# Spectral mixing and SoLU on one core: quarter-array stays of four units, a later booked landing of transposes, an earlier rank for the last product

## Chip, cores, metric

One core of one Trainium2 chip. The metric is device time in microseconds (us) of one execution; the kernel before was run three times (median 1628.03, 1625.98 to 1630.09), and one more execution was profiled.

## What is computed

```python
X = np.fft.rfft(x, axis=1)                    # x: 8 x 3136 x 256, float32
Yr = X.real @ w_r - X.imag @ w_i + b_r
Yi = X.real @ w_i + X.imag @ w_r + b_i
Y  = soft_threshold(Yr, 0.01) + 1j * soft_threshold(Yi, 0.01)
t  = np.fft.irfft(Y, n=3136, axis=1).reshape(25088, 256)
h  = t @ w_in                                 # 256 -> 1024
solu = h * softmax(h)
ln = (solu - mean) / sqrt(var + 1e-6) * g_ln
out = ln @ w_out                              # 1024 -> 256
```

## The kernel before

Each of the 8 batches goes through two Fourier steps forward (`fwd1`, `fwd2`), the mixing product with threshold (`mix`), two steps back (`inv1`, `inv2`), and then a product with `w_in`, an activation and a product with `w_out`. Products of single precision are made of three float16 products on TensorE: high part by high, high by low, low by high.

**Front.** `fwd1` of batches 2 to 7 works on quarters of the array (49 rows by 64 columns, weights `fa16_s`) with four PSUM banks a stay; batches 0 and 1 use single precision (`fwd1_plain`, weights `fa_s`). Results go to DRAM and come back regrouped. `fwd2`, `mix` and `inv1` work on 13 units a batch: 12 units of two frequency pairs and a last, smaller one. `inv1` contracts over 64 rows, so that two products lie in the array at once, one on each half of its rows (weights `gb`). In batches 1 to 7 it takes two units in one uninterrupted group, 24 matmuls into two banks, and writes one `zout` tile (two buffers), which goes to DRAM in one transfer; `yh` and `yl`, the halves of a mixed unit, have four buffers each. `inv2` brings rows into a ring (`ring_hi`, `ring_lo`) as 128-row tiles of the output.

**Back.** 24 or 25 tiles of 128 rows a batch, 196 in all. `moe_head`: 12 matmuls of 512 columns into two banks (`ph`), row maximum, exponential and product into `u` (four buffers). `moe_turn`: `u` is split into `lh` (ScalarE) and `ll` (GpSimd), two buffers each, and both are transposed by DMA (SyncE's queue) into `th` and `tl`, three buffers each. `moe_tail`: 16 matmuls of 256 columns with `th`, then 8 with `tl`, into one `po` bank; scaled, stored.

**Order.** All instructions are recorded first, and a planner (`Plan.order`, line 351) then writes out the order of every engine by hand; the chip follows that order and waits only on semaphores. The planner books a length for each operation. On each engine it takes, among the operations that could start within 50 ns of the earliest, the one of lowest key, then of earliest recording. Batch `b`'s tile `n` has the keys `first + n` (head), `first + n + 0.5` (turn) and `first + n + 1.5` (tail), where `first` counts the tiles of the batches before. `front_b(b + 1)` is spread over the same keys: unit `n` of `fwd2` and `mix(n - 1)` at `key + n * step`, and the `inv1` of units `u - 1, u` at step `u + 3`; a step is some 1.2 tiles, and 1.0 tile in batch 1. A transpose is booked with 1.6 us of the queue, 1.5 us of a common bus and 2.0 us to land; what depends on it may start then, and the buffers that it reads (`lh`, `ll`) come free then, in the book (lines 414 to 426). Banks: 8 in all, at most 5 for the front (`pf`), 5 for heads, 2 for tails (line 478). Matmuls on parts of the array are booked with 100 ns to enter such a stay from the full array and 220 ns otherwise.

Of the kernel before, what the change touches and what calls it, by code (L numbers as in the profile page):

```python
# [12 lines left out]
F32 = mybir.dt.float32  # L13
F32R = mybir.dt.float32r
BF16 = mybir.dt.bfloat16
F16 = mybir.dt.float16
# [18 lines left out]
LOW = 2.0**11  # L35
# [207 lines left out]
class Plan:  # L243
# [60 lines left out]
    def weigh(self, op, name, args, kw, ins, outs):  # L304
        if name == "dma_start":
            v = next(v for v in (*outs, *ins) if not isinstance(v, DramView))
            size = (v.rows[1] - v.rows[0]) * v.cells.size * mybir.dt.size(v.dtype)
            cross = kw.get("transpose", False)
            op.length += 1600.0 if cross else 430.0
            op.moved += 1500.0 if cross else size / 270.0  # L310
        elif op.engine == "tensor":
            moving = ins[-1]
            n = moving.cells.size * (4 if moving.dtype == F32 else 1) * 0.42 + 1
            name = ins[0].tile.kw["name"]
            op.split = 2 if "gb" in name else 4 if name == "fa16_s" else 1
# [35 lines left out]
    def order(self):  # L351
# [38 lines left out]
        while len(done) < len(self.ops):  # L390
# [22 lines left out]
                port = op.end  # L413
            if op.moved:
                bus = max(bus, op.end) + op.moved
                op.end = bus + 2000.0
            for t in op.tiles:
                if t.owner is None:
                    t.owner = op
# [39 lines left out]
def fft_mix_solu_kernel(ctx: ExitStack, tc, x, w_r, w_i, b_r, b_i, w_in, w_out, g_ln, fa, fbf, fsf, iaf, fa16, fb, fs, gb, gs, ia, out):  # L459
# [29 lines left out]
        return t  # L489

    nc.key = -300
    fa_s = load([N1, N1], fa, "fa_s")
    nc.key = 0
    ident = const.tile([P, P], F32, name="ident")
    ones = const.tile([P, P], F32, name="ones")
# [66 lines left out]
    def set_scales(b):  # L562
# [19 lines left out]
        nc.vector.tensor_scalar(un[:, 3:], un[:, :1], 1.0 / S_SCALE, sc[:, 1:2], ALU.mult, ALU.mult)  # L582
        nc.vector.tensor_scalar(sc[:, 2:3], sc[:, 1:2], LAM, None, ALU.mult)
        nc.vector.tensor_scalar(sc[:, 3:4], sc[:, 1:2], -LAM, None, ALU.mult)
        bias_y = fp.tile([P, 2, D], F32, name="bias_y", bufs=2)
        nc.vector.tensor_scalar(bias_y, bias_t, sc[:, 1:2], None, ALU.mult)
        nc.vector.tensor_scalar(un[:, 2:3], un[:, 3:], w_un, None, ALU.mult)
        scales[b] = dict(
            x=sc[:, 0:1], X=sc[:, 4:], lam=(sc[:, 2:3], sc[:, 3:4]), mix=un[:, 2:3], bias=bias_y, y=un[:, 1:2]
        )  # L590
        if b:
            set_h_scale(b)

# [207 lines left out]
    def mix(b, u):  # L801
        n, _ = unit_size(u)
        half = 2 * N2
        M = n * half
        t = mix_split(b, u) if b else mix_first(u)
        c = fp.tile([P, 2, D], F32, name="yc", bufs=2)
        up, down = scales[b]["lam"]
# [5 lines left out]
        else:  # L813
            nc.vector.tensor_scalar(c[:M], t[:M], up[:M], down[:M], ALU.min, ALU.max)
        nc.gpsimd.tensor_sub(y[:M], t[:M], c[:M])
        yh = fp.tile([P, 2, D], F16, name="yh", bufs=4)
        yl = fp.tile([P, 2, D], F16, name="yl", bufs=4)
        nc.scalar.copy(yh[:M], y[:M])
        nc.gpsimd.tensor_sub(yl[:M], y[:M], yh[:M])
        Ys[b, u] = yh, yl  # L820
# [1 line left out]
    def inv1(b, u0, u1):  # L822


        n, _ = unit_size(u0)
        half = 2 * N2
        K = half * n
        g, gi = divmod(2 * u0, QG)
        part, dtype = ((2, D), F16) if b >= PLAIN_Z else ((D,), F32)
        if n == 1:  # L830
            zo, gi = fp.tile([K, 1, *part], dtype, name="zs", bufs=1), 0
        else:
            if gi == 0:
                zouts[b] = fp.tile([P, QG, *part], dtype, name="zout")
            zo = zouts[b]
        w = u1 - u0
        pz = [front_psum(b) for _ in range(n)]
        nc.reserve(zo[:, gi : gi + n * w])
        with nc.together():
            for u in range(u0, u1):  # L840
                yh, yl = Ys.pop((b, u))
                for k, (t, j) in enumerate(((yh, 0), (yl, 0), (yh, 1))):
                    for ri in range(2):
                        for i in range(n):
                            rows = slice(i * half, (i + 1) * half)
                            gw = gs_s[:, ri, j] if n == 1 else gb_s[g][rows, u % 2, ri, j]
                            nc.tensor.matmul(
                                pz[i][:K, (u - u0) * D : (u - u0 + 1) * D], gw, t[rows, ri], start=k + ri == 0, stop=k + ri == 3
                            )
        m = n * w  # L850
        for i in range(n):
            pv = pz[i][:K, : w * D].rearrange("p (u e) -> p u e", u=w)
            if b < PLAIN_Z:
                zv = zo[:, gi : gi + m].rearrange("p (u i) e -> p u i e", i=n)[:, :, i]
                nc.scalar.activation(zv, pv, AF.Copy, scale=Z_SCALE)
                continue
            zv = zo[:, gi : gi + m].rearrange("p (u i) t e -> p u i t e", i=n)[:, :, i]
            nc.scalar.activation(zv[:, :, 0], pv, AF.Copy, scale=Z_SCALE)
            nc.vector.scalar_tensor_tensor(zv[:, :, 1], zv[:, :, 0], -LOW, pv, ALU.mult, ALU.add)
        if b >= PLAIN_Z:  # L860
            zo = zo.rearrange("p q t e -> p q (t e)")
        if n == 1:
            nc.sync.dma_start(s2[b][4 * Q :].rearrange("c (n m) -> (c n) m", n=N2), zo[:, 0])
        else:
            v = s2[b][: 4 * Q].rearrange("(q c) m -> q (c m)", c=4).rearrange("q (r m) -> r q m", r=P)
            nc.sync.dma_start(v[:, g * QG + gi : g * QG + gi + m], zo[:, gi : gi + m])

# [315 lines left out]

    def front_b(b, key, step):

        lag = 4 if b == 0 else 3
        for n in range(NU + lag):
            nc.key = key + n * step  # L1190
            for fn, u in ((fwd2, n), (mix, n - 1)):
# [3 lines left out]
            if u == NU - 1 or 0 <= u < NU and b == 0:  # L1195

                inv1(b, u, u + 1)
            elif 0 < u < NU and u % 2:
                inv1(b, u - 1, u + 1)

    nc.key = -140
    set_scales(0)
# [17 lines left out]
    for b in range(B):  # L1220
# [9 lines left out]
        for n in range(L):  # L1230
# [5 lines left out]
            heads.append(moe_head((b, n if n < 24 else None)))  # L1236
            nc.key = first + n + 0.5
            turned.append(moe_turn(*heads.pop(0)))
            nc.key = first + n + 1.5
            moe_tail(*turned.pop(0))  # L1240
        first += L
    nc.issue(tc)
# [24 lines left out]
```

## Time and profile before

| | |
|---|---|
| median of three runs | 1628.03 us |
| the profiled execution | 1626.85 us, its span 1625.1 us |
| TensorE matmul busy | 1564.6 us (96%) |
| VectorE / ScalarE / GpSimd busy | 1332.9 (82%) / 1242.8 (76%) / 1121.0 (69%) us |
| DMA engines, mean busy share | 78.8% |
| TensorE in the chain that ended last | 79% |

All operations are recorded through one helper, so that every line number in the profile is 349; groups are told apart by their tiles' names (`po<-wout,th` is the tail's first part). Durations of matmuls overlap by their pipeline: the pace is read from starts.

### The profile page before, as it was taken

How to read it: one execution, taken by the hardware profiler on the slowest of the kernel's cores; microseconds unless marked ns; L12 is line 12 of the kernel's file. 1: busy time of each engine (PE TensorE's matmuls, PEld its weight loads, DVE VectorE, ACT ScalarE, POOL GpSimd, SP SyncE). 2: the span in 40 equal slices, each digit the busy share in tenths (PEclk: the TensorE clock that was granted, in tenths of full speed). 3: DMA queues.
4: the chain of work that ended last, by engine and by line, in shares of the span. 5: the costliest groups of instructions: out<-in, count | busy, mean ns of one | idle time of the engine just before them, and what ended most of it. 6: DMA issues, size and time to landing. Idle time of an engine off the chain costs nothing.

```text
span 1625.1 us, 39102 instructions
## 1 busy us (share of the span) xinstructions
PE 1564.6 (96%) x13328; PEld 1107.1 (68%) x13328; DVE 1332.9 (82%) x3423; ACT 1242.8 (76%) x2576; POOL 1121.0 (69%) x1890
## 2 busy tenths in 40 slices
PE   5979999899999999999999999999999999999998
PEld 3645877468765777667766687666776577776675
DVE  4779899988998888887978789788887879877774
ACT  4667777886788867897778877788678877788886
POOL 0555777657875688667876578766876677776775
PEclk8989999999999999999999999999999999999999
DMA  8878987898898975789669995789857994587765
GB/s 235 272 226 209 230 230 173 205 221 216 200 210 169 209 175 127 161 185 213 161 126 171 190 200 132 147 177 205 188 124 148 181 198 124 128 156 146 141 130 110
DMA packets 540649, 290.30 MB, mean 179 GB/s; under 512 B 429660, under 2 KB 505982, under 8 KB 540450
## 3 DMA queue, kind: packets, MB, share of 16 engines
q1 hardware_dynamic: 540450, 287.81, 78.8%
q8 instruction: 104, 1.70, 0.4%
q14 instruction: 95, 0.78, 0.1%
HBM read 107.88 MB, written 77.07 MB: 114 GB/s over the span
## 4 chain that ended last, share of the span: by engine, by line
PE 79%; DMA 7%; DVE 5%; ACT 4%; issue 2%; POOL 1%; SPq 1%; DVEq 0%; ACTq 0%; POOLq 0%
PE po L349 27%; PE ph L349 24%; PE pf L349 23%; PE pb L349 4%; DMA th<-lh 3%; DMA tl<-ll 2%; DVE u L349 1%; ACT u L349 1%; SPq L349 1%; DVE nm L349 1%; POOL ll L349 1%; ACT junk L349 1%; DVE xl L349 1%; ACT lh L349 0%; DMA zt<-s2f 0%
## 5 line engine op out<-in xcount | busy, mean ns | idle before, releaser
L349 POOL TENSOR_TENSOR ll<-u,lh 128x1024 f16<-128x1024 f32 x196 | 420.6, 2146 | 136.5 <-ACT lh L349 111.1
L349 PE MATMUL po<-wout,th 128*128 128x256 f16 x3136 | 379.7, 275 | 18.2 <-DMA th<-lh 18.0
L349 PEld LDWEIGHTS <-th 128*128 128x128 f16 x3136 | 305.1, 99 | 88.7 <-DMA th<-lh 26.3
L349 ACT ACTIVATE u<-ph,m,hsb 128x512 f32<-128x512 f32 x384 | 296.1, 777 | 75.0 <-DVE m L349 74.7
L349 DVE TENSOR_REDUCE nm<-ph 128x1 f32<-128x512 f32 x392 | 265.8, 686 | 91.9 <-PE ph L349 90.5
L349 DVE SCALAR_TENSOR_TENSOR u<-ph,ch,u 128x512 f32<-128x512 f32 x392 | 282.2, 748 | 28.5 <-ACT u L349 12.7
L349 PE MATMUL ph<-win_hi,ring_hi 128*128 128x512 f16 x768 | 291.9, 380 | 1.2 <-DVE u L349 1.2
L349 PE MATMUL ph<-win_low,ring_lo 128*128 128x512 f16 x768 | 291.5, 380 | 0.0
L349 PE MATMUL ph<-win_lo,ring_hi 128*128 128x512 f16 x768 | 291.5, 380 | 0.0
L349 ACT CAST lh<-u 128x1024 f16<-128x1024 f32 x196 | 205.4, 1048 | 78.3 <-DVE u L349 74.4
L349 PEld LDWEIGHTS <-ring_hi 128*128 128x128 f16 x1536 | 145.7, 98 | 137.8 <-issue 10.8
L349 ACT ACTIVATE junk<-u,total 128x1024 bf16<-128x1024 f32 x196 | 226.0, 1153 | 6.4 <-POOL total L349 6.3
L349 PE MATMUL po<-wout,tl 128*128 128x256 f16 x1568 | 203.9, 273 | 9.1 <-DMA tl<-ll 9.1
L349 POOL TENSOR_TENSOR y<-yt,yc 128x512 f32<-128x512 f32 (+1 forms) x104 | 136.6, 1314 | 69.8 <-ACT yt L349 33.1
L349 PEld LDWEIGHTS <-tl 128*128 128x128 f16 x1568 | 150.6, 98 | 42.8 <-DMA tl<-ll 12.7
L349 PE MATMUL pf<-w_hi,Xl 128*128 128x256 f16 (+1 forms) x546 | 148.8, 273 | 1.1 <-DVE Xl L349 1.1
L349 PE MATMUL pf<-w_hi,Xh 128*128 128x256 f16 (+1 forms) x546 | 149.2, 273 | 0.0
L349 PE MATMUL pf<-w_lo,Xh 128*128 128x256 f16 (+1 forms) x546 | 148.8, 273 | 0.0
L349 POOL TENSOR_TENSOR yl<-y,yh 128x512 f16<-128x512 f32 (+1 forms) x104 | 124.0, 1193 | 34.0 <-ACT yh L349 32.3
L349 PEld LDWEIGHTS <-ring_lo 128*128 128x128 f16 x768 | 75.2, 98 | 91.0 <-DVE peaks L349 0.3
L349 ACT ACTIVATE o<-po,r 128x256 f32<-128x256 f32 x196 | 93.4, 476 | 56.2 <-PE po L349 42.6
L349 PEld LDWEIGHTS <-Xh 128*128 128x128 f16 (+1 forms) x1196 | 113.5, 99 | 26.4 <-issue 1.9
(197 smaller groups left out, 2843.1 us busy)
## 6 DMA issues: line engine op xcount, KB each, us to landing
xt<-in_x_dram SPq DMA_DIRECT2D x60, 392.0 KB
zt<-s SPq DMA_DIRECT2D x56, 392.0 KB
s<-zout SPq DMA_DIRECT2D x42, 512.0 KB
xt<-in_x_dram SPq DMA_DIRECT2D x96, 192.0 KB
s<-av SPq DMA_DIRECT2D x96, 192.0 KB
bin<-s SPq DMA_DIRECT2D x36, 512.0 KB
out_dram<-o SPq DMA_DIRECT2D x128, 96.0 KB
out_dram<-o SPq DMA_DIRECT2D x136, 64.0 KB
```

Source lines behind the costliest of these rows:

```text
L349: getattr(engine, name)(*args, **kw)
```

## The change

Four things change. In the book, a transpose lands 3.0 us later than before (on a bus without a queue, from 5.1 to 8.1 us after its issue begins); nothing on the chip is told of it. The tail's key falls from `first + n + 1.5` to `first + n + 1`. In batches 1 to 7, `inv1` takes four units (48 matmuls, four banks, both `zout` buffers) where it took two, and a stay is placed one step after its last unit's `mix`, where it was two; the two transfers of a stay are issued after it, one after the other. Buffers make room: `yh` and `yl` get five in place of four, `bias_y` one in place of two (it is now made when a batch's first unit is mixed, not with the batch's scales), and `fa_s` moves into the place of `Xs`, of which there is one.

```diff
@@ Plan.weigh
             op.length += 1600.0 if cross else 430.0
             op.moved += 1500.0 if cross else size / 270.0
+            op.late = 3000.0 if cross else 0.0
@@ Plan.order
                 bus = max(bus, op.end) + op.moved
-                op.end = bus + 2000.0
+                op.end = bus + 2000.0 + op.late
@@ fft_mix_solu_kernel
-    fa_s = load([N1, N1], fa, "fa_s")
+    fa_s = fp.tile([P, ND, 2, 2 * N2], F32, name="Xs", bufs=1).rearrange("p h i c -> p (h i c)")[:N1, :N1]
+    nc.sync.dma_start(fa_s, fa)
@@ set_scales
-        bias_y = fp.tile([P, 2, D], F32, name="bias_y", bufs=2)
-        nc.vector.tensor_scalar(bias_y, bias_t, sc[:, 1:2], None, ALU.mult)
@@ mix
+        if u == 0:
+            scales[b]["bias"] = fp.tile([P, 2, D], F32, name="bias_y", bufs=1)
+            nc.vector.tensor_scalar(scales[b]["bias"], bias_t, scales[b]["up"], None, ALU.mult)
...
-        yh = fp.tile([P, 2, D], F16, name="yh", bufs=4)
-        yl = fp.tile([P, 2, D], F16, name="yl", bufs=4)
+        yh = fp.tile([P, 2, D], F16, name="yh", bufs=5)
+        yl = fp.tile([P, 2, D], F16, name="yl", bufs=5)
@@ inv1
-        w = u1 - u0
-        pz = [front_psum(b) for _ in range(n)]
-        nc.reserve(zo[:, gi : gi + n * w])
+        work = []
+        for u2 in range(u0, u1, 2):
...
+            us = range(u2, min(u2 + 2, u1))
+            work.append((g, gi, zo, us, [front_psum(b) for _ in range(n)]))
+        nc.reserve(*(zo[:, gi : gi + n * len(us)] for _, gi, zo, us, _ in work))
         with nc.together():
-            for u in range(u0, u1):
+            for g, _, _, us, pz in work:
+                for u in us:
...
+        for g, gi, zo, us, pz in work:
...
@@ front_b
-        lag = 4 if b == 0 else 3
+        lag = 4 if b == 0 else 2
...
-            elif 0 < u < NU and u % 2:
-                inv1(b, u - 1, u + 1)
+            elif 0 < u < NU and u % 4 == 3:
+                inv1(b, u - 3, u + 1)
@@ the loop over tiles
-            nc.key = first + n + 1.5
+            nc.key = first + n + 1
             moe_tail(*turned.pop(0))
```

## Rows read from the trace of the kernel before

**Rows 1.** Waits of TensorE, whole run: total us, times, longest us.
```profile
PE po L349 <- DMA th<-lh: 18.0, 14, 4.6
...
PE po L349 <- DMA tl<-ll: 9.1, 10, 1.5
...
PE ph L349 <- DVE u L349: 1.2, 3, 0.6
...
PE pf L349 <- DVE u L349: 0.6, 2, 0.3
```

**Rows 2.** Stretches: us, busy us by engine, clock, DMA share, GB/s.
```profile
120.00:330.00 210.00, 201.37 (x1544) 143.91 (x1544) 191.19 (x499) 155.15 (x320) 143.29 (x237) 0.97 0.87 209
330.00:1600.00 1270.00, 1250.40 (x11142) 894.55 (x11141) 1056.09 (x2757) 1006.07 (x2095) 916.75 (x1584) 1.00 0.79 169
...
1600.00:1626.00 26.00, 18.67 (x128) 12.88 (x126) 8.98 (x27) 12.88 (x26) 12.51 (x27) 0.89 0.49 102
```

**Rows 3.** Waits of TensorE, 120 to 330 us.
```profile
PE po L349 <- DMA th<-lh: 6.8, 3, 4.6
...
PE po L349 <- DMA tl<-ll: 0.6, 1, 0.6
```

**Rows 4.** Waits of TensorE, 330 to 1600 us.
```profile
PE po L349 <- DMA th<-lh: 9.4, 10, 2.6
PE po L349 <- DMA tl<-ll: 8.1, 8, 1.5
```

**Rows 5.** Waits of TensorE, 1600 us to the end.
```profile
PE po L349 <- DMA th<-lh: 1.8, 1, 1.8
PE po L349 <- DMA tl<-ll: 0.4, 1, 0.4
```

**Rows 6.** Chain that ended last: start us, us from a transpose's issue to its landing.
```profile
1124.77 7.06 DMA tl<-ll
...
1281.09 4.57 DMA th<-lh
```

**Rows 7.** Timeline of TensorE, 573 to 584 us: start us, us, instructions.
```profile
573.64 1.05 PE L349 MATMUL po<-wout,tl 128*128 128x256 f16 x8 [1.39 <-DMA tl<-ll]
574.52 0.27 PE L349 MATMUL pf<-w_hi,Xh 128*128 128x256 f16 x1
...
582.27 0.27 PE L349 MATMUL pf<-w_hi,Xl 128*128 128x256 f16 x1
582.48 0.39 PE L349 MATMUL pf<-yh,gb 64*128 64x256 f16 x4
...
583.58 0.38 PE L349 MATMUL pf<-yh,gb 64*128 64x256 f16 x4
583.90 0.84 PE L349 MATMUL pf<-fb,bin 128*128 128x128 f16 x12
```

**Rows 8.** Groups of TensorE by shape: busy us, mean ns, idle before.
```profile
L349 PE MATMUL pf<-yh,gb 64*128 64x256 f16 x672 | 57.7, 270 | 0.0
...
L349 PE MATMUL pf<-xh,fa_s 49*64 49x512 f16 x384 | 30.8, 392 | 0.6 <-DVE u L349 0.6
```

**Rows 9.** Timeline of TensorE around 914 us.
```profile
913.76 3.53 PE L349 MATMUL po<-wout,th 128*128 128x256 f16 x16 [2.32 <-DMA th<-lh]
```

**Rows 10.** Stretches at the lower clock, columns as in Rows 2.
```profile
319.70:326.60 6.90, 5.13 (x38) 4.14 (x39) 2.25 (x13) 2.90 (x6) 3.68 (x6) 0.51 1.08 222
913.60:917.10 3.50, 3.34 (x16) 2.40 (x17) 3.50 (x18) 2.58 (x7) 1.57 (x6) 0.51 1.03 193
1299.30:1302.80 3.50, 3.50 (x31) 1.45 (x29) 3.11 (x12) 3.50 (x9) 2.18 (x4) 0.51 1.19 138
```

**Rows 11.** Groups on GpSimd: busy us, mean ns, idle before.
```profile
L349 POOL TENSOR_TENSOR ll<-u,lh 128x1024 f16<-128x1024 f32 x196 | 420.6, 2146 | 136.5 <-ACT lh L349 111.1 <-DMA tl<-ll 20.5 <-ACT u L349 2.9
...
L349 POOL TENSOR_TENSOR yl<-y,yh 128x512 f16<-128x512 f32 (+1 forms) x104 | 124.0, 1193 | 34.0 <-ACT yh L349 32.3
```

**Rows 12.** A group on VectorE, columns as in Rows 11.
```profile
L349 DVE TENSOR_SCALAR bias_y<-bias_t,sc 128x512 f32<-128x512 f32 x8 | 3.8, 476 | 0.0
```

More of the change, by code (lines that the diff above doesn't have):

```diff
@@ L584, in set_scales @@
         nc.vector.tensor_scalar(sc[:, 3:4], sc[:, 1:2], -LAM, None, ALU.mult)
-        bias_y = fp.tile([P, 2, D], F32, name="bias_y", bufs=2)
-        nc.vector.tensor_scalar(bias_y, bias_t, sc[:, 1:2], None, ALU.mult)
         nc.vector.tensor_scalar(un[:, 2:3], un[:, 3:], w_un, None, ALU.mult)
-        scales[b] = dict(
-            x=sc[:, 0:1], X=sc[:, 4:], lam=(sc[:, 2:3], sc[:, 3:4]), mix=un[:, 2:3], bias=bias_y, y=un[:, 1:2]
-        )
+        scales[b] = dict(x=sc[:, 0:1], X=sc[:, 4:], lam=(sc[:, 2:3], sc[:, 3:4]), mix=un[:, 2:3], y=un[:, 1:2], up=sc[:, 1:2])
         if b:
@@ L827, in inv1 @@
         K = half * n
-        g, gi = divmod(2 * u0, QG)
         part, dtype = ((2, D), F16) if b >= PLAIN_Z else ((D,), F32)
[L830 to L835, printed above, removed]
-        w = u1 - u0
-        pz = [front_psum(b) for _ in range(n)]
-        nc.reserve(zo[:, gi : gi + n * w])
-        with nc.together():
-            for u in range(u0, u1):
[L841 to L866, printed above, removed]
+        work = []
+        for u2 in range(u0, u1, 2):
+            g, gi = divmod(2 * u2, QG)
+            if n == 1:
+                zo, gi = fp.tile([K, 1, *part], dtype, name="zs", bufs=1), 0
+            else:
+                if gi == 0:
+                    zouts[b] = fp.tile([P, QG, *part], dtype, name="zout")
+                zo = zouts[b]
+            us = range(u2, min(u2 + 2, u1))
+            work.append((g, gi, zo, us, [front_psum(b) for _ in range(n)]))
@@ new lines, in inv1 @@
+        nc.reserve(*(zo[:, gi : gi + n * len(us)] for _, gi, zo, us, _ in work))
+        with nc.together():
+            for g, _, _, us, pz in work:
+                for u in us:
+                    yh, yl = Ys.pop((b, u))
+                    for k, (t, j) in enumerate(((yh, 0), (yl, 0), (yh, 1))):
+                        for ri in range(2):
+                            for i in range(n):
+                                rows = slice(i * half, (i + 1) * half)
+                                gw = gs_s[:, ri, j] if n == 1 else gb_s[g][rows, u % 2, ri, j]
+                                at = slice((u - us[0]) * D, (u - us[0] + 1) * D)
+                                nc.tensor.matmul(pz[i][:K, at], gw, t[rows, ri], start=k + ri == 0, stop=k + ri == 3)
@@ new lines, in inv1 @@
+        for g, gi, zo, us, pz in work:
+            w = len(us)
+            m = n * w
+            for i in range(n):
+                pv = pz[i][:K, : w * D].rearrange("p (u e) -> p u e", u=w)
+                if b < PLAIN_Z:
+                    zv = zo[:, gi : gi + m].rearrange("p (u i) e -> p u i e", i=n)[:, :, i]
+                    nc.scalar.activation(zv, pv, AF.Copy, scale=Z_SCALE)
+                    continue
+                zv = zo[:, gi : gi + m].rearrange("p (u i) t e -> p u i t e", i=n)[:, :, i]
+                nc.scalar.activation(zv[:, :, 0], pv, AF.Copy, scale=Z_SCALE)
+                nc.vector.scalar_tensor_tensor(zv[:, :, 1], zv[:, :, 0], -LOW, pv, ALU.mult, ALU.add)
+            if b >= PLAIN_Z:
+                zo = zo.rearrange("p q t e -> p q (t e)")
+            if n == 1:
+                nc.sync.dma_start(s2[b][4 * Q :].rearrange("c (n m) -> (c n) m", n=N2), zo[:, 0])
+            else:
+                v = s2[b][: 4 * Q].rearrange("(q c) m -> q (c m)", c=4).rearrange("q (r m) -> r q m", r=P)
+                nc.sync.dma_start(v[:, g * QG + gi : g * QG + gi + m], zo[:, gi : gi + m])
```

## The prediction

> **What bounds the kernel now.** I read the busy time by stretches first. From 330 us to 1600 us TensorE works 1250.4 of 1270 us, 98.5%, and no other engine is over 84% there [rows 2]. So TensorE's order bounds the kernel, and two things can shorten the run: fewer or cheaper matmuls, or less of the 19.6 us in which TensorE stands still in that stretch. The list of its waits names these: 9.4 us for `th` and 8.1 us for `tl`, 17.5 us in 18 waits [rows 4]. Two other stretches count less. From 120 us to 330 us TensorE waits 7.4 us for transposes [rows 3], but VectorE is busy 191.2 of 210 us there [rows 2], so an earlier matmul helps only as far as VectorE keeps up. After 1600 us the waits are 2.2 us [rows 5], and only the last tiles' own chain is left, with no work to put in. Together that is the 27.1 us of the whole run [rows 1].
>
> Why the waits exist: the book lets a transpose land 1.6 + 1.5 + 2.0 = 5.1 us after its issue begins, if the bus is free, and the planner ranks an old tail before other work. Where TensorE waited, the chain shows 4.57 to 7.06 us from issue to landing (these two and nine between) [rows 6]. The tail stands at the place in TensorE's order where the book says that it may run, the chip is up to 2 us later, and what stands behind it waits too. The timeline shows what that was: at 573.64 the `tl` part starts after 1.39 us of waiting, and twelve mixing matmuls follow at 574.52 without a wait [rows 7]. They were most likely ready; the order alone kept them back.
>
> **Part 1: the later landing.** With 3.0 us more in the book, a tail is placed 8.1 us after its transpose or later, beyond the longest landing of the chain. Each wait but one is shorter than 3.0 us [rows 3, 4], so all but 4.6 - 3.0 = 1.6 us could go, if the planner has other work for TensorE in that time. Bounds: nothing at one end; at the other 27.1 - 2.2 = 24.9 us, and the clock with it. [...]
> What I take: in the long stretch, two waits (2.32 us at 914 [rows 9], and the longest, 2.6 [rows 4]) come after a run of heads, with little but that tail left in the order; 4.9 of the 17.5 us. I count half of these, 2.4, and all of the other 12.6, which resemble the one in rows 7: 15.0 us. Engines that were hidden come late next (VectorE's 1056 of 1270 us leaves holes only on the mean), so I keep two thirds: **-10.0**. Of the clock's two stretches after 330 us, 6.84 us at half speed, 3.4 us are lost and I take half: **-1.7**. Before 330 us I take a quarter, since VectorE binds: a quarter of 7.4 + 2.6 us: **-2.5**.
> What is booked later too: `lh` and `ll` come free 3.0 us later. An `ll` buffer is then held for 2.15 us of GpSimd [rows 11] and 8.1 us of landing, 10.3 us, and two buffers allow a tile each 5.1 us. A tile needs about 2.6 us for its head (twelve matmuls of 512 columns, twice 0.11 us each) and as much for its tail (24 at 0.11, from 573.64 to 574.52 for eight [rows 7]), 5.2 us. That is just enough; on the chip the real landing frees the buffer, so I count 0. GpSimd already waited 20.5 us for `tl` before it could write `ll` [rows 11]; these waits become shorter.
>
> **Part 2: the tail's rank.** Half a tile lower, the tail of tile n comes before the head of n + 1 where both could start; before, the head came first. But a tail is ready 3.0 us later in the book, so mostly the head is gone by then. No instruction is added. Bounds: 0, and the slower rival below. I take 0.
>
> **Part 3: four units in a stay.** Batches 1 to 7 have 672 / 16 = 42 stays of two units [rows 8]; 21 remain. A switch is seen in the starts: 256-column matmuls follow each other by 0.11 us (0.88 us for eight at 573.64), but from the last mixing matmul at 582.27 to the first of the stay at 582.48 it is 0.21, so 0.10 more. Inside, ten pairs go from 582.48 to 583.58, 0.11 each; the last two pairs would free the array at 583.80, and the next work starts at 583.90, again 0.10 [rows 7]. 21 stays by 0.20 us: **-4.2**. TensorE is the bound, so this counts in full.
> [...]
> A stay takes four banks at once, of five for the front. The nearest row is `fwd1`, which already does so: 384 / 16 = 24 stays [rows 8]. TensorE's waits for a bank that VectorE's `u` frees are 1.2 + 0.6 = 1.8 us in all [rows 1]. Bounds: 0, and the longest single wait, 0.6 us, at each of the 21 stays, 12.6. I take the mean of `fwd1`, 21 by 1.8 / 24: **+1.6**.
> A stay follows its last unit's `mix` by one step in place of two (1.2 tiles of some 1500 / 196 us, 9 us), and needs its `yl`, the last of the chain on GpSimd. TensorE never waited for `yh` or `yl` before. Bounds: 0, and one `yl` of 1.19 us [rows 11] a stay, 25 us. A step is longer than the chain, so I take a value near the lower end: **+1.0**. With five `yh` buffers, the copy for the second unit after a stay has to wait for that stay on ScalarE, with splits and exponentials of tiles behind it; the planner sees this and orders round it: 0, bounded by one stay's matmuls, 2.6 us, after two of the three long stays of each of seven batches, 36 us at most.
> SyncE issues the same 42 stores, now by twos, and transposes behind a pair start one issue later, some 0.5 us. The 3.0 us cover that; without them it would be late tails again.
>
> **Part 4: buffers.** `bias_y` is the same eight instructions of 0.48 us on VectorE [rows 12], now just ahead of the first mixing result of a batch; one batch's units end long before the next one's begin. `fa_s` in the place of `Xs` delays nothing that does not wait anyway: the first `Xs` needs all of batch 1's `fwd1_plain`, the last user of `fa_s`. Both 0.
>
> **The sum.** -10.0 - 1.7 - 2.5 - 4.2 + 1.6 + 1.0 = -15.8 us. The profiled execution took 1626.85 us, 1.75 more than its span, and lies 1.2 us under the median. 1626.85 - 15.8 = 1611.0 by that execution, and 1628.0 - 15.8 = 1612.2 by the median; I say **1612**. Its own range is 1603 to 1620.
>
> **Rivals.** (a) *Everything goes*: all 24.9 us of waits, the 6.0 us of clock, 4.2 of switches: -35.1, **1593**. For it: most waits are under 1.7 us, and TensorE has other work almost always. Against: the waits after a run of heads have nothing else behind them, and VectorE binds before 330 us.
> (b) *The order hardly changes*: the half tile of rank gives back what the 3.0 us take, or the book has no other work, and the tails stay where they are. Then only the switches go: -4.2 + 2.6 = -1.6, **1626**. For it: the waits lie in clusters where the DMA share is high and fronts are through. Against: the mixing matmuls behind the wait of rows 7.
> (c) *Slower: tails before heads starve VectorE.* In 120 to 330 us VectorE is at 91%, and its work for a tile starts from a head. If the lower rank puts a tail of 2.6 us before a head at each of batch 0's 24 tiles, and VectorE can fill half of it, that is 24 by 1.3 = 31 us; less the 4.2 and 10.0 gained elsewhere it is +17, and +7 if it strikes two thirds of the tiles: I price it between, at +12, **1640**. It decides from the point where the loss exceeds 14 us, about 11 such tiles. Against: TensorE has 201.4 of 210 us there, so the order shifts waits rather than adding work.
> (d) *Banks*: 0.6 us at each four-bank stay, +12.6 in place of +1.6, gives **1623**. [...] `fwd1`'s rows speak against: 1.8 us in 24 such stays.
>
> **Chances.** Forecast 0.46, (a) 0.13, (b) 0.16, (c) 0.17, (d) 0.08. A measurement of this kernel can tell about 0.3%, 4.9 us, from no change. Faster by more than that: the forecast, (a), and half of (d), whose 1623 lies on the line: 0.63. Within: (b) and the other half, less a little of (b) beyond each side: 0.19. Slower: (c) and that little: 0.18. Range: 1596 to 1636; it leaves out most of (a) below and over half of (c) above, and holds the costs' bounds as far as one of them alone goes.
>
> **What would show each step.** [...] Wrong: waits for `yl`, or for VectorE's `u` beyond 3 us; VectorE's waits for `ph` in 120 to 330 us longer by 10 us or more; or transposes that land later than 8 us because a pair of stores is ahead of them. What would make the prediction wrong as a whole is a hole at a change of batches that is no wait for a tail, since I count none.

## The result and the profile after

Twelve runs of the changed kernel have a median of 1633.95 us (1630.19 to 1640.64), twelve of the kernel before 1625.52 us (1622.88 to 1630.09): a ratio of 1.0048, 95% interval 1.0034 to 1.0062. The change makes the kernel slower by half a per cent, some 8 us. The time lies in the range of the prediction, but the sign was wrong: 1612, faster, had been forecast. The profiled execution took 1636.71 us.

The first two lines of the page of after are its span and the busy time of its engines:

```profile
span 1634.9 us, 38927 instructions
PE 1566.4 (96%) x13328; PEld 1111.9 (68%) x13328; DVE 1326.3 (81%) x3423; ACT 1236.6 (76%) x2576; POOL 1110.5 (68%) x1890
```

TensorE's work is the same. The first two stretches of [rows 2] in after, and then those at the lower clock (columns: stretch, its us, busy us of PE, PEld, DVE, ACT and POOL, clock, DMA share, GB/s):

```profile
120.00:330.00 210.00, 201.95 (x1520) 142.85 (x1520) 187.19 (x486) 152.82 (x316) 139.89 (x228) 0.96 0.86 203
330.00:1600.00 1270.00, 1243.62 (x11095) 895.07 (x11094) 1045.39 (x2747) 994.94 (x2086) 905.50 (x1580) 0.99 0.79 169
```
```profile
154.60:161.40 6.80, 5.67 (x21) 3.04 (x21) 6.17 (x20) 4.68 (x12) 6.53 (x12) 0.50 0.70 168
318.40:325.20 6.80, 6.16 (x33) 4.69 (x34) 6.09 (x16) 5.02 (x9) 4.97 (x6) 0.50 0.98 197
355.90:359.30 3.40, 3.40 (x22) 2.60 (x20) 1.21 (x3) 1.83 (x5) 0.66 (x4) 0.51 1.19 292
908.90:912.30 3.40, 3.40 (x20) 2.35 (x18) 2.22 (x12) 3.28 (x6) 2.27 (x8) 0.50 0.87 172
960.10:963.50 3.40, 3.40 (x13) 1.66 (x11) 1.69 (x4) 2.75 (x7) 0.89 (x3) 0.50 0.93 194
1123.90:1127.30 3.40, 3.40 (x11) 1.21 (x10) 2.59 (x9) 3.40 (x8) 2.44 (x11) 0.51 1.56 233
```

In the long stretch TensorE stands still for 1270 - 1243.6 = 26.4 us, 6.8 more than in [rows 2], and between 130 and 1600 us six stretches have a granted clock of 0.50 or 0.51 where [rows 10] has three. The waits of TensorE in the whole run (total us, times, longest us), answering to [rows 1], tell what it stood still for:

```profile
PE pf L350 <- DMA bin<-s: 10.8, 5, 3.0
...
PE pf L350 <- DVE u L350: 8.1, 7, 1.9
PE ph L350 <- DVE u L350: 6.5, 4, 3.2
PE po L350 <- DMA tl<-ll: 3.1, 2, 1.9
PE po L350 <- DVE u L350: 1.5, 1, 1.5
...
PE po L350 <- DMA th<-lh: 1.2, 2, 1.0
```

The waits for transposes are all but gone, 27.1 us before and 3.1 + 1.2 = 4.3 now. In their place stand two others: 10.8 us for `bin`, the rows that `fwd2` of a new batch reads, for which TensorE never waited after 120 us before; and 8.1 + 6.5 + 1.5 = 16.1 us for `u`, which is VectorE freeing PSUM banks. The timeline shows one of the first kind, TensorE's rows and then SyncE's (start us, us, instructions; in brackets the idle time before and what ended it):

```profile
753.01 1.04 PE L350 MATMUL po<-wout,tl 128*128 128x256 f16 x8
756.29 0.84 PE L350 MATMUL pf<-fb,bin 128*128 128x128 f16 x12 [2.24 <-DMA bin<-s]
756.97 1.91 PE L350 MATMUL po<-wout,th 128*128 128x256 f16 x16
```
```profile
750.77 1.23 SPq L350 DMA_TRANSPOSE th<-lh  x1
752.06 1.16 SPq L350 DMA_DIRECT2D bin<-s  x2
```

The tail at 753.01 doesn't wait any more. Behind it stands the first `fwd2` of a batch, and what waits behind that is a tail: the mirror image of [rows 7]. TensorE comes to this `fwd2` at 754.05, 2.0 us after the issue of its load began, and starts it 4.2 us after. The book allows such a load 0.43 us of the queue, 1.9 us of the bus (512 KB by 270) and 2.0 us to land, 4.4 us on a free bus; so the load was not slow, it was issued late. SyncE had issued without a pause of more than 0.1 us since 745.20, three transposes (4.7 us) and four stores. The five waits for `bin` begin at 352, 552, 754, 956 and 1357 us, each at the first `fwd2` of a batch, and end 4.2 to 4.9 us after their load's issue began.

The mode switches did what was forecast. A stay of after:

```profile
608.48 0.27 PE L350 MATMUL pf<-w_hi,Xl 128*128 128x256 f16 x1
608.68 0.39 PE L350 MATMUL pf<-yh,gb 64*128 64x256 f16 x4
...
611.09 0.38 PE L350 MATMUL pf<-yh,gb 64*128 64x256 f16 x4
611.41 0.28 PE L350 MATMUL pf<-w_hi,Xh 128*128 128x256 f16 x1
```

From 608.48 to 608.68 it is 0.20 us, 0.09 over the pace of 0.11. From 608.68 to 611.09 lie 22 pairs, 0.11 us each; two more end at 611.31, and the next work starts at 611.41, 0.10 later. That is one entry and one exit for 48 matmuls, where [rows 7] has them for 24.

The account, from the starts of TensorE's matmuls after 120 us: every start that comes later than the shape's pace allows is counted, and lateness over 0.15 us is put down as a wait. How much goes under each head depends on the pace taken, so these are estimates: waits +9 to +11 us, the lower clock +4 to +5, small excesses within the work -4 to -5. The last lies nearly all at and around the stays, where matmuls with `gb` fall from 4.5 us of excess to 2.1 and those of `mix` from 4.3 to 2.2: -4.5. Together it is +9.9, and the spans differ by 1634.9 - 1625.1 = 9.8.

### The profile page after: what moved, and what is told of

It reads as the page before. It is cut to its first block, busy times and chain, and to the rows that moved or that the text cites. A ratio compares the mean times of both kernels' runs of the same rounds, so it can differ in the third digit from the quotient of the medians.

```text
span 1634.9 us, 38927 instructions
## 1 busy us (share of the span) xinstructions
PE 1566.4 (96%) x13328; PEld 1111.9 (68%) x13328; DVE 1326.3 (81%) x3423; ACT 1236.6 (76%) x2576; POOL 1110.5 (68%) x1890
## 5 line engine op out<-in xcount | busy, mean ns | idle before, releaser
L350 PEld LDWEIGHTS <-ring_hi 128*128 128x128 f16 x1536 | 147.1, 98 | 141.3 <-issue 16.3
L350 ACT ACTIVATE junk<-u,total 128x1024 bf16<-128x1024 f32 x196 | 226.1, 1153 | 13.9 <-POOL total L350 13.5
```

The lines of the kernel that those rows point to most:

```text
L350: getattr(engine, name)(*args, **kw)
```

## The experiments

The expectations name five theories. M: the waits move to what is next late. F: the stays of four units do harm. R: any change of the book reshuffles the order, and the time scatters. B: TensorE's order binds, and a wait for a tail is pure loss. L: other inputs are as late as the tails.

### The parts one by one

The later landing alone:

```diff
+            op.late = 3000.0 if cross else 0.0
-                op.end = bus + 2000.0
+                op.end = bus + 2000.0 + op.late
```

> The kernel before with one part alone: a transpose lands 3.0 us later in the planner's book. Theory M (waits move): the tails' 27.1 us of waits fall under 6 us as in the changed kernel, but heads run further ahead and TensorE waits for banks that VectorE frees (u) and for the first load of a batch (bin) instead, 15 us or more together; time 1626 to 1636, ratio 1.000 to 1.006. Theory F (the four-unit stays did the harm): this part alone gains what the prediction counted, 1608 to 1616, ratio 0.990 to 0.994. Theory R (any change of the book reshuffles the whole order and the time scatters): anywhere from 1618 to 1640, with no fixed relation to which waits go.

The rank alone:

```diff
-            nc.key = first + n + 1.5
+            nc.key = first + n + 1
```

> The kernel before with one part alone: the tail's key is first + n + 1. Nothing lands later in the book, so a tail comes before the head of the next tile where both could start. Theory M: the tails' waits stay at 20 to 35 us or grow, bank waits stay under 4 us; 1624 to 1634, ratio 0.999 to 1.005. Theory F: no effect, ratio 0.998 to 1.002. Theory R: a scatter of up to 8 us either way.

Both of these edits:

```diff
+            op.late = 3000.0 if cross else 0.0
-                op.end = bus + 2000.0
+                op.end = bus + 2000.0 + op.late
-            nc.key = first + n + 1.5
+            nc.key = first + n + 1
```

> The kernel before with the two changes of the book (landing 3.0 us later, tail's key half a tile lower) and stays of two units as before. Theory M: like the changed kernel without the gain of its switches, 1632 to 1642, ratio 1.004 to 1.010, with waits for VectorE's u and for bin of 15 us or more. Theory F: 1608 to 1616, ratio 0.990 to 0.994. Theory R: not the sum of the two parts alone; anywhere from 1618 to 1640.

The stays of four with their buffers, without either edit (the hunks of `fft_mix_solu_kernel`, `set_scales`, `mix`, `inv1` and `front_b`):

```diff
-        lag = 4 if b == 0 else 3
+        lag = 4 if b == 0 else 2
-            elif 0 < u < NU and u % 2:
-                inv1(b, u - 1, u + 1)
+            elif 0 < u < NU and u % 4 == 3:
+                inv1(b, u - 3, u + 1)
...
```

> The changed kernel with the book and the tail's key of before: the four-unit stays, the shorter way from mix to inv1 and the moved buffers alone. Theory M: the switches' 4.2 us are gained and the tails' waits stay at 20 to 30 us: 1618 to 1624, ratio 0.995 to 0.999. Theory F: the stays hold up the front, 1632 to 1640, ratio 1.004 to 1.009, with waits for banks or for yl at the stays. Theory R: 1618 to 1640.

Measured against the kernel before: later landing 1633.21 us, 1.0042 [1.0029, 1.0056]; rank 1641.18, 1.0085 [1.0066, 1.0103]; both 1640.31, 1.0079 [1.0059, 1.0099]; stays of four 1647.22, 1.0126 [1.0103, 1.0149]. Each part alone is slower, and they don't add: 7.5 + 15.5 + 21.5 = 44.5 us one by one, 8.4 together. Later landing and both edits fell into M's ranges; the rank alone and the stays alone came out above every range that was stated. The stays of four save the switches and still come out slowest. A part whose loss vanishes when another is added has no price of its own; so the next question was what an edit that means nothing costs.

### Edits that mean nothing

Four on the kernel before: 10 ns more to land for every transfer in the book; 1 ns more for a sight of ScalarE (the book's allowance until another engine sees its result); 52 ns in place of 50 within which the planner may choose; 1 ns more for a sight of VectorE.

```diff
-                op.end = bus + 2000.0
+                op.end = bus + 2010.0
```

> The kernel before with no part of the change: every transfer is booked to land 10 ns later (2010 in place of 2000), which means nothing to the chip; about half of TensorE's order changes all the same. Theory R (any change of the book reshuffles the order, and the order of before is a low point of that scatter): 1629 to 1645, ratio 1.002 to 1.012. Theory M (the loss comes from what the parts do): within 3 us of before, ratio 0.998 to 1.002.

```diff
-    SEEN = dict(tensor=250.0, vector=160.0, scalar=190.0, gpsimd=160.0, sync=90.0)
+    SEEN = dict(tensor=250.0, vector=160.0, scalar=191.0, gpsimd=160.0, sync=90.0)
```

> The kernel before with no part of the change: the planner's allowance for the sight of a ScalarE result is 191 ns in place of 190. About 15% of TensorE's order changes. Theory R: 1627 to 1640, ratio 1.001 to 1.009. Theory M: ratio 0.998 to 1.002.

```diff
-    PATIENCE = 50.0
+    PATIENCE = 52.0
```

> The kernel before with no part of the change: the planner's patience is 52 ns in place of 50. About 22% of TensorE's order changes. Theory R: 1627 to 1640, ratio 1.001 to 1.009, and another value than the two other changes of this kind. Theory M: ratio 0.998 to 1.002.

```diff
-    SEEN = dict(tensor=250.0, vector=160.0, scalar=190.0, gpsimd=160.0, sync=90.0)
+    SEEN = dict(tensor=250.0, vector=161.0, scalar=190.0, gpsimd=160.0, sync=90.0)
```

> The kernel before with 161 ns in place of 160 for the sight of a VectorE result; a quarter of TensorE's order changes. Theory R: 1624 to 1640; with the three others of its kind the mean stays above before. Theory M: ratio 0.998 to 1.002.

And two on the kernel after:

```diff
-                op.end = bus + 2000.0 + op.late
+                op.end = bus + 2010.0 + op.late
```

> The changed kernel with every transfer booked to land another 10 ns later, which means nothing to the chip; a third of TensorE's order changes. Theory R: as wide a scatter as that of before: 1624 to 1645, ratio to the kernel before 0.999 to 1.012. Theory M: the change's loss is its own and stays within 3 us: 1631 to 1637.

```diff
-    PATIENCE = 50.0
+    PATIENCE = 52.0
```

> The changed kernel with a patience of 52 ns in place of 50; six tenths of TensorE's order change. Theory R: 1624 to 1645 and not the value of the run with 10 ns. Theory M: 1631 to 1637.

Each ratio is to the kernel before as run beside that version (medians 1625 to 1626 us); the waits are TensorE's from 120 to 1600 us, in us, summed over the rows of the view of waits, from one profiled execution each:

| kernel | us | ratio | for `th`, `tl` | for `bin` | for `u` | all waits |
|---|---|---|---|---|---|---|
| before | 1625.5 | 1 | 24.9 | 0 | 1.8 | 27.8 |
| before, patience 52 | 1623.77 | 1.0004 [0.9990, 1.0017] | 25.2 | 0 | 2.2 | 28.8 |
| before, ScalarE 1 ns | 1633.51 | 1.0044 [1.0030, 1.0057] | 23.1 | 2.1 | 1.9 | 33.6 |
| before, all 10 ns | 1637.60 | 1.0072 [1.0055, 1.0089] | 17.3 | 1.1 | 3.8 | 35.2 |
| before, VectorE 1 ns | 1639.06 | 1.0076 [1.0052, 1.0099] | 15.8 | 0.6 | 7.4 | 32.0 |
| rank alone | 1641.18 | 1.0085 [1.0066, 1.0103] | 25.8 | 2.6 | 2.7 | 37.5 |
| stays of four alone | 1647.22 | 1.0126 [1.0103, 1.0149] | 20.4 | 3.1 | 8.8 | 44.7 |
| later landing alone | 1633.21 | 1.0042 [1.0029, 1.0056] | 0 | 9.4 | 7.6 | 30.8 |
| landing and rank | 1640.31 | 1.0079 [1.0059, 1.0099] | 0 | 12.5 | 7.9 | 39.4 |
| after | 1633.95 | 1.0048 [1.0034, 1.0062] | 1.0 | 11.6 | 16.1 | 33.7 |
| after, all 10 ns | 1635.32 | 1.0048 [1.0032, 1.0063] | 1.1 | 9.7 | 13.5 | 36.8 |
| after, patience 52 | 1645.54 | 1.0111 [1.0090, 1.0133] | 5.1 | 8.5 | 12.9 | 40.9 |

Two things follow. The times scatter, as R said: edits without meaning moved the kernel before by 0.04 (not to be told from 0), 0.44, 0.72 and 0.76% and the one after by 0.00 and 0.63%, while the change itself is +0.48%. Only patience 52 on the kernel before fell to M, and patience 52 on the one after came out just above R's range. None of these edits was faster than before; its order is a low point of the scatter. Five plans of the kernel before (itself among them) have a mean ratio of 1.0039, three of after 1.0069; with a scatter of 0.3 to 0.4% among each, the two families can't be told apart. So the change's loss is of R's size, and its sign can't be told from that of one draw. The stays of four alone, at +1.26%, lie above every edit without meaning on the kernel before, so that some harm of their own (F) is not excluded; together with the other parts they show none.

The waits don't scatter like that. All five kernels that book the later landing wait 8.5 to 12.5 us for `bin`, the seven others 0 to 3.1. All three with everything wait 12.9 to 16.1 us for `u`, all others 1.8 to 8.8. So the exchange of waits, M, belongs to the change: the later landing alone brings that of tails for `bin`, and of the versions here only those with all parts have the whole of that for `u`.

### What a wait for a tail is worth

To separate the wait from the order, a second pass of the plan took the starts of the first as its keys and booked transposes 1.5 us later:

```diff
+        self.late = 0.0
+        self.order()
+        self.again(1500.0)
         order = self.order()
-                op.end = bus + 2000.0
+                op.end = bus + 2000.0 + (self.late if op.cross else 0.0)
```

> The order of before is planned first and kept: in a second pass each operation's key is its start in the first, and a transpose is booked to land 1.5 us later. So the tails slide back on TensorE while nine tenths of the rest of its order stay. (With 0 in place of 1.5 us the order of before comes out unchanged.) Theory R: without the reshuffle the prediction's first part holds: the tails' waits fall from 27 to under 14 us, nothing of that size takes their place, 1610 to 1619, ratio 0.990 to 0.996. Theory M: the waits for tails fall but waits for bin and for banks come in their place, 1624 to 1634, ratio 0.999 to 1.005.

1637.05 us, 1.0072 [1.0054, 1.0089], above both ranges: it re-planned too, within the scatter, and waits for `zt` (6.7 us), `u`, `Xl` and `ring_hi` came up as the tails' fell from 24.9 to 7.2. It settles nothing that the table doesn't. The next pair leaves the order as it is, instruction by instruction, and takes the cause away: tails multiply by a slice of `win_hi` in place of `th` and `tl`, and the transposes are still issued. Its output is another product; only its time is of use, and that holds for every version below with tails free.

```diff
+                    if op.engine == "tensor" and args[0].tile.kw["name"] == "po" and args[1].tile.kw["name"] in ("th", "tl"):
+                        f = args[1].path[-1][1][0][1]
+                        args = (args[0], self.stand[:, 0, f * 128 : (f + 1) * 128], *args[2:])
...
+    nc.stand = win_hi
```

> The order of the kernel before, kept to the last instruction; but the tails multiply by a constant tile (a part of win_hi) in place of th and tl, so that no tail waits for a transpose. The transposes are still issued and nobody waits for them: the product with w_out is another, its work the same. Theory B (TensorE's order binds and the tails' waits are pure loss, as the prediction had it): the 24.9 us and up to 6 us of clock go, 1594 to 1604, ratio 0.981 to 0.987. Theory L (other inputs are as late as the transposes, so that TensorE waits for the next of them): 1614 to 1625, ratio 0.993 to 1.000, with 12 us or more of new waits for bin, zt, banks or VectorE.

1621.21 us, 0.9984 [0.9969, 0.9999]. All 27.1 us of waits for transposes are gone, in the very order of before, and 3 to 4 us are gained (2.6 by the ratio, with 0.2 to 5.0 as its interval, 3.8 by the medians). The list of TensorE's waits of this kernel from 330 to 1600 us (total, times, longest), and its long stretch, columns as above, ahead of the same stretch of before:

```profile
PE pf L352 <- DVE last_lo L352: 3.9, 2, 2.7
PE pf L352 <- DVE u L352: 3.1, 4, 2.1
PE pf L352 <- DMA bin<-s: 2.9, 2, 1.7
PE pf L352 <- DMA zt<-s: 2.7, 3, 1.9
PE pf L352 <- DVE Xl L352: 1.6, 2, 1.1
PE po L352 <- DVE u L352: 1.3, 1, 1.3
```
```profile
330.00:1560.00 1230.00, 1211.90 (x10828) 869.30 (x10829) 1028.16 (x2670) 973.25 (x2033) 891.52 (x1533) 0.99 0.80 170
330.00:1560.00 1230.00, 1210.40 (x10831) 866.57 (x10830) 1026.21 (x2667) 973.68 (x2030) 888.07 (x1527) 1.00 0.79 170
```

None of these was a wait of before, but for 0.6 and 1.2 us for `u` [rows 1] and 1.1 for `Xl`. From 330 to 1560 us TensorE still stands still for 1230 - 1211.9 = 18.1 us, against 19.6 before. Two of the places, start us, us, instructions:

```profile
738.10 0.84 PE L352 MATMUL pf<-fb,bin 128*128 128x128 f16 x12 [1.70 <-DMA bin<-s]
...
1296.03 0.62 PE L352 MATMUL pf<-xh,fa_s 49*64 49x512 f16 x6 [2.65 <-DVE last_lo L352]
```

Shortly ahead of this `fwd2` and this `fwd1`, the kernel before waits 1.50 us for `tl` (to 740.21) and 2.59 for `th` (to 1298.11), and then not for them. As the order is the same to the last of 13328 matmuls, the two executions can be laid side by side: the version with free tails leads by 1.8 us at 130 us, ahead of the first wait, by 7.3 at 330, 2.1 at 400, 4.9 at 900 and 3.3 at 1600. L holds: loads of the front and VectorE's results come just behind the tails, and a wait for a tail mostly hides one of those. The same on the kernel after:

```diff
+                    if op.engine == "tensor" and args[0].tile.kw["name"] == "po" and args[1].tile.kw["name"] in ("th", "tl"):
...
+    nc.stand = win_hi
```

> The order of the changed kernel, kept to the last instruction; the tails multiply by a constant tile as in the run before, the transposes are issued and nobody waits for them. The changed kernel waits 4.3 us for transposes. Theory B and theory L alike: 2 to 6 us less than the changed kernel, 1627 to 1633, ratio to the kernel before 1.001 to 1.005; the waits for bin (10.8 us) and for VectorE's u (16 us) stay. It tells how much of the changed kernel's loss has nothing to do with tails.

1630.97 us, 1.0036 [1.0021, 1.0051], 0.12% or 2 us under the change itself, less than the two intervals can tell apart: its 4.3 us of waits for tails were worth little or nothing.

### What makes everything late

Next, the same two kernels (tails free) without the 392 transposes, with the order of before and with that of after:

```diff
+                    if kw.get("transpose"):
+                        continue
```

> As the run on the order of before with free tails, and the 392 transposes are not issued at all (left out, with their traffic; SyncE's queue is that much shorter). Theory B: no more than 4 us below the run that still issues them. Theory L with the DMA engines as the cause: what had taken the place of the tails' waits goes with the traffic, 1594 to 1604, at least 10 us below the run that issues them.

```diff
                 for name, args, kw in op.calls:
+                    if kw.get("transpose"):
+                        continue
```

> As the run on the order of the changed kernel with free tails, and the 392 transposes are not issued at all. If the waits for bin come from transposes that share the DMA engines with the loads, they fall from 10.8 us to under 3 and the time to 1615 to 1623; if they come from the queue's order or from the front's own chain, they stay above 8 us and the time within 4 us of the run that issues them. Bank waits for VectorE's u stay near 16 us either way.

Order of before: 1596.18 us, 0.9820 [0.9792, 0.9848], as L said. Order of after: 1603.25, 0.9862 [0.9838, 0.9885], below both of its ranges. The stretch from 330 to 1560 us with the order of before, and TensorE's waits from 120 to 1600 us with it and then with that of after:

```profile
330.00:1560.00 1230.00, 1225.07 (x10992) 882.04 (x10990) 1037.83 (x2705) 986.10 (x2065) 904.56 (x1557) 1.00 0.35 100
```
```profile
PE pf L354 <- DVE v L354: 3.6, 2, 1.8
PE ph L354 <- DVE u L354: 1.2, 3, 0.6
...
PE po L354 <- DVE u L354: 0.9, 3, 0.5
PE pf L354 <- DVE u L354: 0.8, 3, 0.3
```
```profile
PE ph L355 <- DVE u L355: 5.5, 3, 3.5
PE pf L355 <- DVE u L355: 4.0, 4, 1.4
PE po L355 <- DVE u L355: 1.8, 2, 1.5
...
PE pf L355 <- DMA bin<-s1f: 0.5, 1, 0.5
```

Beyond what the waits for tails were worth, 1621.21 - 1596.18 = 25.0 us go with the order of before and 1630.97 - 1603.25 = 27.7 with that of after; the DMA share falls from 0.80 to 0.35, and the waits for loads go with it. So `bin` is late because of what transposes bring with them. Most of the waits for `u` are not: of 15.3 us in the order of after with tails free, 5.5 + 4.0 + 1.8 = 11.3 stay, against 1.2 + 0.9 + 0.8 = 2.9 with the order of before. That is +8.4, less the 4.5 saved by fewer switches +3.9, and the two spans, 1601.5 and 1596.8, differ by 4.7 (the medians by 7.1). Without any transposes the order of after is slower by its waits for banks.

What do transposes bring: the time of SyncE, which issues all the DMAs, or the traffic? Summed over SyncE's rows of the timeline, before issues for 1073.9 of 1625 us, 550 of these for transposes (392 of 1.40); without them it is 481.6. In place of each transpose three plain transfers of 1 KB, and then two, give SyncE work with nearly no traffic (tails free in both, as above):

```diff
                     if kw.get("transpose"):
+                        for j in range(3):
+                            self.nc.sync.dma_start(args[0].placed()[:16, j, :32], args[1].placed()[:16, j * 32 : j * 32 + 32])
                         continue
```

> The order of the kernel before, tails on a constant tile, and in place of each of the 392 transposes three transfers of 1 KB each (16 rows of 32 numbers), so that SyncE's queue is about as busy as with the transposes (1.26 us for one), while the DMA engines have next to nothing of their traffic. If what takes the place of the tails' waits comes from traffic on the DMA engines, the time stays near the run without transposes, 1593 to 1602; if it comes from SyncE's queue, it goes back to the run that issues them, 1616 to 1625, with waits for bin, zt and VectorE.

```diff
-                        for j in range(3):
+                        for j in range(2):
```

> As the run with three transfers of 1 KB in place of each transpose (order of before, tails on a constant tile), with two: SyncE's issues then come to about 482 + 392 by 2 by 0.59 = 945 us, a little under the 1074 us of the kernel before; the run with three had 1228 us, the one with none 482. If SyncE's queue is what holds the other inputs up, the time lies between the run without transposes and the run with them: 1604 to 1621. If the queue matters only above what the kernel has and the traffic is the cause below that, it stays at 1594 to 1602.

Three: 1672.99 us, 1.0283 [1.0261, 1.0305], with SyncE issuing for 1228 us. Two: 1599.08, 0.9835 [0.9804, 0.9866], with 969 us. The timeline of SyncE, first with three:

```profile
553.85 2.27 SPq L349 DMA_DIRECT2D th<-lh  x3
556.22 1.81 SPq L349 DMA_DIRECT2D tl<-ll  x3
```
```profile
553.16 1.21 SPq L349 DMA_DIRECT2D th<-lh  x2
```

TensorE's largest waits from 330 to 1600 us, with three and then the largest with two, and one wait for `bin` with three:

```profile
PE pf L356 <- DMA zt<-s: 9.1, 4, 3.5
PE pf L356 <- DMA bin<-s: 8.8, 6, 2.8
PE pf L356 <- DVE last_lo L356: 7.4, 3, 3.7
```
```profile
PE pf L356 <- DVE v L356: 1.7, 1, 1.7
```
```profile
973.35 0.84 PE L356 MATMUL pf<-fb,bin 128*128 128x128 f16 x12 [2.84 <-DMA bin<-s]
```

With 969 us of issues and hardly any traffic (DMA share 0.36 from 330 to 1560 us) the kernel is within 3 us of the one without transposes; with 1228 us and the same share it is 74 us slower than that, beyond both ranges of its expectation. The wait to 973.35 ends 4.1 us after its load's issue began, and five of the six for `bin` in this run end after 4.1 to 4.4 (one after 5.6). In after, with a share of 0.79, it was 4.2 to 4.9. So those loads land about as fast without the transposes' traffic, and what made them late in after is mostly the time at which SyncE came to issue them. This is read from the traces; no run took only SyncE's time or only the traffic from the order of after. To find on which side the 1074 us of before lie, with all of its traffic and its order, ScalarE issued every second store of an output tile:

```diff
-        order = self.order()
+        order, stored = self.order(), []
...
+                    out = op.engine == "sync" and op.tiles[0].kw["name"] == "o"
+                    if out:
+                        stored.append(op.tiles[0])
+                    by = self.nc.scalar if out and stored.count(op.tiles[0]) == 2 else engine
...
-                    getattr(engine, name)(*args, **kw)
+                    getattr(by, name)(*args, **kw)
```

> The kernel before, its order kept, and the second of the two stores of each output tile is issued from ScalarE's queue in place of SyncE's; nothing is left out. It takes some 100 us from SyncE's 1074 us of issues and lays up to as much on ScalarE (1243 of 1625 us busy). If SyncE's queue holds the inputs up, TensorE's waits for th and tl fall from 27 to under 18 us and the time to 1610 to 1621, ratio 0.990 to 0.998. If it does not, or ScalarE loses as much: 1623 to 1640.

1621.10 us, 0.9987 [0.9971, 1.0002], between its two ranges: no change that can be told, with SyncE's issues down to 976 us. TensorE's waits for transposes fell all the same, from 24.9 to 8.5 us between 120 and 1600 us. TensorE's first waits there, 330 to 1600 us:

```profile
PE pf L353 <- DVE Xl L353: 4.9, 9, 1.1
PE po L353 <- DMA th<-lh: 3.9, 5, 1.8
PE pf L353 <- ACT Xh L353: 3.1, 5, 1.2
```

In that stretch waits for `tl` are gone and those for `Xl` and `Xh` stand there: M once more. At equal work for SyncE, 976 and 969 us, the kernel with transposes has 0.9987 and the one with two tiny transfers 0.9835, 1.5% or 25 us apart, of which the tails' own waits are 3 to 4. So some 21 us of the order of before go with the transposes' traffic or with the time that they take to land, which holds `lh` and `ll` (GpSimd waited 20.5 us for it before it could write `ll` [rows 11]); these two were not separated. (The run with 976 us also has ScalarE issue for 78 us, so that the 21 may be a little less.) So 98 us less of SyncE's issues, with all the traffic, gained nothing that can be told, while 259 us more of them, from 969 to 1228, with hardly any, cost 74.

## Why the prediction was wrong, point by point

**The tails' waits, -10.0: the step that failed.** That they would go was right: of 27.1 us 4.3 were left, and the median from a transpose's issue to the first use of `th` rose from 5.9 to 8.7 us, by 2.8 where 3.0 had been booked. What failed is the step from there to the time: "They were most likely ready; the order alone kept them back", and two thirds kept for engines that come late next. In before's own order the removal of all these waits, at no cost, was worth 3 to 4 us, a tenth to a seventh of the 27.1. I had looked at what stands behind one wait [rows 7] and judged all by it. The twelve mixing matmuls there were ready: with free tails they don't wait either, though the next ones wait 0.85 us, at 581.35, for `Xl`. Elsewhere the loads of the next front and VectorE's results were as late as the tail. And when the planner moves a tail back, it moves something else ahead: a `fwd2` for whose load SyncE was late.

The reason given for the waits was wrong too. The range of 4.57 to 7.06 us from issue to landing leaves out part of the chain: it has 18 transposes, 3.08 to 7.06 us, and at the wait of [rows 9], to 913.76, this one:

```profile
910.43 3.28 DMA th<-lh
```

Of the 23 waits of before over 0.25 us, 16 with 16.3 of 26.9 us ended less than the booked 5.1 us after their transpose's issue began. There it was the issue that came late, not the landing; 3.0 us more in the book cover that as well, which is luck. The prediction named what would make it wrong: a hole at a change of batches that is no wait for a tail. Five of them are 10.8 us.

**The clock, -1.7.** Wrong in sign. After 330 us four stretches of 3.4 us at a granted clock of 0.50 to 0.51 cost 6.8 us where two cost 3.4, an estimate at half the pace: from 908.86 the 16 matmuls of a tail follow each other by 0.21 us, where 0.11 is the pace. Each follows a moved wait by 0.4 to 1.0 us: 2.98 and 2.56 us for `bin` that ended at 355.50 and 959.10, 1.73 and 1.94 us for `u` that ended at 908.32 and 1123.10. But a wait of 2.24 us for `bin`, to 756.29, was followed by none. The clock went with the waits, not one for one. The 3.4 and 2.6 us of clock in the forecast and the 6.0 in rival (a) are halves of TensorE's work in [rows 10]; no run shows them as a gain. With free tails and the order of before, where no wait for a tail is left, the clock from 330 to 1560 us was 0.99, and 1.00 before.

**Before 330 us, -2.5.** Nothing came. TensorE was at the lower clock for 6.8 us from 154.6, 1.1 us ahead of the end of its longest wait for a bank (3.23 us, to 155.74), and again from 318.4. In before, too, the stretch from 319.70 [rows 10] began within the longest wait (4.59 us, to 321.47) and not after it.

**The switches, -4.2.** Right: 4.5 us, read from the starts; the rows of after show 0.09 and 0.10 for a switch again.

**Banks, +1.6.** Mis-sized, and in another place. No four-unit stay of `inv1` waited for a bank. But all waits for `u` rose from 1.8 to 16.1 us, at the stays of `fwd1`, at `inv2` (908.32), at heads and at a tail; the row of after that answers to [rows 8]:

```profile
L350 PE MATMUL pf<-xh,fa_s 49*64 49x512 f16 x384 | 31.4, 383 | 4.5 <-DVE u L350 4.2 <-ACT o L350 0.2
```

0.6 us stood there. Rival (d) had waits for banks and nearly their size (12.6), though at the wrong stays. Taking the mean of `fwd1` in the old order for a price was the error, and it was misread: of the 1.8 us, 1.2 stood at heads [rows 1], and `fwd1` had 0.6. These waits went mostly with the order, which the change altered: without transposes they are 2.9 us in the order of before and 11.3 in that of after.

**`yl`, +1.0, and the rank, 0.** No wait for `yl` in after. The rank alone came out at +0.85%, little above the edits that mean nothing. Rival (b), 1626, did not happen: the order changed, and the tails moved. Rival (c), 1640, came nearest in time and had the sign, by luck: tails before heads did not starve VectorE, whose wait for `ph` from 120 to 330 us rose by 2.5 us, not by 10; the row of after, then that of before:

```profile
DVE nm L350 <- PE ph L350: 4.4, 7, 1.3
```
```profile
DVE nm L349 <- PE ph L349: 1.9, 2, 1.3
```

**The missing term.** The sum had none for re-planning. An edit of 1 ns in the book moved the time by 0.44 and 0.76%, 7 and 12 us, as much as the terms that I added up; a forecast of -15.8 with a range that came only from costs was too sure of its sign. What stays open is why the order of before is a low point. That it was the best of many drawn is likely, but no run here shows it. Open too is whether traffic or landing makes the 21 us that transposes cost beyond SyncE's time and the tails' waits. No version here that computes the same output beats the kernel before beyond doubt.

## What to carry to other kernels

Where a planner writes the order, first measure how far the time moves on an edit that means nothing; a part of a change that is worth less than that can be neither credited nor blamed by its time, only by waits that come and go with it in every variant. What a wait is worth is read by pinning the order and taking its cause away: here 27 us of waits on an engine 98.5% busy were worth 3 to 4, since the next inputs were as late. So before a wait is counted as gain, look at every one of its places for what comes in next, above all at changes of batches, where all five waits for `bin` stood here.

## What the hardware showed that I had not expected

A plain transfer of 1 KB took SyncE a median of 0.58 us to issue (588 and 392 of them, into `th`), a store of 32 to 96 KB of an output tile 0.49 (0.52 on the mean); the smaller size did not make these issues cheaper. From ScalarE the same store took 0.40 us (196 of them). A transpose took 1.40 us on the mean to issue. A load of 512 KB for which TensorE waited was usable 4.2 to 4.9 us after its issue began at a mean DMA share of 0.79, and mostly 4.1 to 4.4 at 0.36. One queue that issued for 969 of 1598 us delayed nothing that can be seen (1599.08 us, and 1596.18 with 482 us of issues), and for 1228 of 1673 us it cost 74 us over that. And 392 transposes, whose absence takes the DMA share of the long stretch from 0.80 to 0.35, make the whole kernel 29 us slower, though TensorE's waits for their results are worth only 3 to 4 of it.
